# Gated linear attention and a gated convolution layer on one Trainium2 core: low parts and state sums on TensorE, weights in twelve parts, unit rows padded to 128, a new plan

## The chip, the cores and the metric

The kernel runs on one core of one Trainium2 chip. The metric is device time in microseconds, the median of several executions. The core's engines work on their own instruction queues, each in order: TensorE (PE; its weight loads are shown apart as PEld), VectorE (DVE), ScalarE (ACT), GpSimd (POOL), and SyncE (SP), which here issues most DMAs.

## The reference

For each of 4 batches and 8 heads a state of 48 x 48 is carried along 768 steps. Its output y, the heads side by side, is the x (768 x 384) of the second half.

```python
state = alpha[:, :, t, :, None] * state + einsum('bhd,bhe->bhde', k[:, :, t], v[:, :, t])
y[:, :, t] = einsum('bhd,bhde->bhe', q[:, :, t], state)

h = maximum(x @ w_in, 0)                  # 384 -> 1024
conv[t] = cw[0]*h[t-1] + cw[1]*h[t] + cw[2]*h[t+1]   # zero outside
out = (h * sigmoid(conv)) @ w_out         # 1024 -> 384
```

## The kernel before

The attention is cut into chunks of 128 time steps: 24 steps (`attn`, L586), six for each batch. Heads are held in two groups of four, on rows 0 to 47 and 64 to 111. Units of one or two chunks are loaded (`load_unit`, L521) and prepared (`prep_unit`, L538) with scans that turn alpha into running products and multiply them into k and q; units 0 to 2 do these multiplies on VectorE, later ones on GpSimd. Units 0 and 1 are the first two chunks of batch 0, unit 2 its chunks 2 and 3, unit 3 its chunks 4 and 5.

A step makes scores `a`, masks them into `at`, transposes k to `kt`, forms the state's update `u`, adds the old state and multiplies by a decay into `sc`, and makes `yp` from `at`, v and the old state. The masks come in three forms (L602 to L616): A multiplies the late half by a mask on VectorE and cuts the early half with two triangles on GpSimd; B multiplies both halves on VectorE (four products, no triangle); C copies on ScalarE and cuts all with four triangles. Before, steps 0 to 3 have form C, 4 and 5 form B, the rest A.

The layer's products run in fp32r with split operands: a value is a high part plus a low part. For x, ScalarE copies the high part out of `yp` and VectorE subtracts it for the low part (L670, L671). Six gathers `x<-x` on SP (L680) then complete the rows of x for a unit.

The weights come as 64-bit floats, in 8 parts of 768 words for each row, two of them staged at a time in `wscr`, which holds one of the two `x2` buffers that batches use. `to_parts` (L684) turns a part into float32 with two ScalarE operations, a clamp, a mask and a shift on VectorE, and an integer add on GpSimd; ScalarE casts the high part, and VectorE (parts 0 to 3) or GpSimd (4 to 7) subtracts it.

The layer (`moe_piece`, L730) works on pieces of 384 time steps, 8 tiles of 128 columns of `w_in` each: nine matmuls `ph`, relu on ScalarE into `h`, the three taps (one on ScalarE, two on VectorE), sigmoid, the product `gf` on VectorE, its high part `g` on ScalarE and low part on GpSimd, then nine matmuls `po`. The first piece needs steps 0 to 3. A `po` result leaves through `ob` and a DMA.

The order on each engine is made by a planner (`Plan.schedule`, L161): it goes through a model of costs, takes the operation of lowest rank among those that could start, and lets no operation start whose rank is over WINDOW (32) above the lowest open one. Ranks come from a formula of turns (L904 to L921) with some values set by hand (L957 to L970). Where the plan leaves TensorE empty before the first `po`, it puts filler matmuls `junk` on zeros (`keep_warm`, L450).

Of the kernel before, what the change touches and what calls it, by code (L numbers as in the profile page):

```python
# [94 lines left out]
class Op:  # L95
    __slots__ = ("eng", "fn", "cost", "lat", "port", "rank", "preds", "succs", "need", "bufs", "allocs", "start", "end", "seq", "xfer", "name", "mode", "base")
# [5 lines left out]
class Plan:  # L102
    ENGINES = ("PE", "DVE", "ACT", "POOL", "SP")

    def __init__(self, window, tol=0.05):
        self.classes = {}
        self.window, self.tol = window, tol
        self.memory = {}
        self.ops, self.bufs = [], []
        self.rank = 0.0  # L110
        self.gap_fill = None
# [16 lines left out]

    def const(self, shape, name, dt=None):

        self.pool(name, 1, int(np.prod(shape[1:])))
        return self.buf(name, shape, name, dt)


    def op(self, eng, fn, reads, writes, cost, port=False, xfer=0.0, name="", mode=None):
# [3 lines left out]
        o.preds, o.succs, o.bufs, o.allocs = set(), [], [], []  # L139
# [170 lines left out]
class Engines:  # L310
# [49 lines left out]
    def act(self, out, a, func, scale=1.0, bias=0.0, accum=None):  # L360
        n = out.n
        cost = (n + 195) / 1200 + (0.1 if isinstance(scale, View) else 0.0) + (0.19 if accum is not None else 0.0)
# [99 lines left out]
def record(nc, akq, akqu, v, vu, wts, out):  # L462
# [27 lines left out]
    plan.pool("small", 4, 48)  # L490
# [9 lines left out]
    ident = plan.const([P, P], "ident")  # L500
    ones = plan.const([R, 1], "ones")
# [13 lines left out]
    def unit_rows(u):  # L515
        b, t0, TU = units[u]
        n = 3 * G * TU
        off = (b * S + t0) * 3 * G * R
        return akqu[off : off + R * n].rearrange("(r x) -> r x", r=R)

    def load_unit(u):  # L521
        b, t0, TU = units[u]
        r = plan.buf("raw", [R, 3 * G * TU], f"akq_{u}")
        L = G * TU
        if u == 0:
            for a in (1, 0, 2):
                cols = slice(a * L, (a + 1) * L)
                E.dma("SP", r[:, cols], unit_rows(u)[:, cols], R * L * 4 / 1000)
        else:
            E.dma("SP", r, unit_rows(u), R * 3 * L * 4 / 1000)  # L530
# [7 lines left out]
    def prep_unit(u, qm, km, am):  # L538
# [4 lines left out]
        flat = raw[u]  # L543
# [32 lines left out]
    def chunk(b, c):  # L576
        u, ci = unit_of[(b, c)]
        TU = units[u][2]
        kq = raw[u].rearrange("p (a t) -> p a t", a=3 * G)
# [6 lines left out]
    def attn(si, form, kte):  # L586
        b, c = steps[si]
        u, ci, ks, qs, vf = chunk(b, c)
        nm = f"{b}_{c}"
        late, early = slice(0, HC), slice(HC, C)  # L590
# [27 lines left out]
        if c < NC - 1:  # L618
            kt_ps = plan.buf("mm", [P, G, R], f"ktp_{nm}", kind="kt")
            E.transposes([(kt_ps[:, g, :], ks[:, g, :]) for g in range(G)], ident[0:R, 0:R], 0.87, f"kt {nm}")  # L620
# [4 lines left out]
            for g in range(G):  # L625
                todo.append((up[0:64, g, :], kt[:, g, 0:64], vf[:, g * D : (g + 1) * D], g == 0, g == G - 1))
                todo.append((up[64:R, g, :], kt[:, g, 64:R], vf[:, (g + G) * D : (g + G + 1) * D], g == 0, g == G - 1))
# [10 lines left out]
        plan.rank += OUT_LAG  # L638
        old = state.get(b)
        yps = []  # L640
        for half in range(2):
            yp = plan.buf("mm", [R, 2, C], f"yp{half}_{nm}", kind="yp")
            for i in range(2):
                g, flip = PAIRS[2 * half + i]
                hs = (g + G, g) if flip else (g, g + G)
                last = c == 0 and i == 1
# [6 lines left out]
        if c > 0:  # L653
            todo = []
            for n in (0, 2, 1, 3):
                yp, i, g, flip = yps[n]
                for j in range(2):
                    rows = slice(64 * j, 64 * j + D)
                    o = 64 * (1 - j) if flip else 64 * j
                    todo.append((yp[o : o + D, i, :], old[rows, g, :], qs[rows, g, :], False, i == 1))  # L660
# [6 lines left out]
        for half in range(2):  # L667
# [3 lines left out]
            E.tt("DVE", at_[:, :, 1, ts], yp[:, :, ::-1], at_[:, :, 0, ts], ALU.subtract)  # L671
# [9 lines left out]
        plan.rank -= OUT_LAG  # L681


    def to_parts(raw64, hi, lo, tmp, full=None, eng="DVE"):  # L684

        lw, hw = raw64[..., 0] if False else raw64[0], raw64[1]
        d, r = tmp
# [7 lines left out]
        if full is not None:  # L695
            E.tt("POOL", full.bitcast(I32), di, ri, ALU.add)
            return
        E.tt("POOL", di, di, ri, ALU.add)
        E.copy("ACT", hi, d)
        E.tt(eng, lo, d, hi, ALU.subtract)  # L700

    WP = 768

    def load_weights(ranks, los):
        w64 = None if wts is None else wts.bitcast(U32).rearrange("p (n two) -> p n two", two=2)
        cut = (lambda a, e: None) if wts is None else (lambda a, e: w64[:, a:e])
        craw = plan.buf("small", [P, 3 * NF, 2], "craw", U32)
        plan.rank = ranks[0]
        E.dma("ACT", craw, cut(8 * WP, 8 * WP + 3 * NF), 24)
        scr = plan.buf("x2", [P, 8, WP], "wscr")  # L710
        for j in range(8):
            plan.rank = ranks[j]
            stg = scr[:, 2 * (j % 2) : 2 * (j % 2) + 2].rearrange("p a w -> p (a w)").bitcast(U32).rearrange("p (w two) -> p w two", two=2)
            tmps = [scr[:, 4 + 2 * (j % 2)], scr[:, 5 + 2 * (j % 2)]]
            i = j // 2 if j % 2 == 0 else 4 + j // 2
            E.dma("SP", stg, cut(i * WP, (i + 1) * WP), 786)
            if j == 0:
                to_parts((craw[:, :, 0], craw[:, :, 1]), None, None, [t[:, 0 : 3 * NF] for t in tmps], full=cw.rearrange("p a f -> p (a f)"))
            if i < 4:
                cs = slice(256 * i, 256 * i + 256)  # L720
                dst = [w[:, :, cs] for w in wi]
                v3 = lambda t: t.rearrange("p (t f) -> p t f", t=3)
                s3 = stg.rearrange("p (t f) two -> p t f two", t=3)
                to_parts((s3[:, :, :, 0], s3[:, :, :, 1]), dst[0], dst[1], [v3(t) for t in tmps], eng=los[j])
            else:
                dst = [w.rearrange("p f m -> p (f m)")[:, (i - 4) * WP : (i - 3) * WP] for w in wo]
                to_parts((stg[:, :, 0], stg[:, :, 1]), dst[0], dst[1], tmps, eng=los[j])
# [303 lines left out]
```

## Time and profile before

| | us |
|---|---|
| median of 3 runs | 364.61 (364.14 to 364.99) |
| profiled execution, first to last instruction (span) | 360.8 |
| TensorE, weight loads, VectorE, ScalarE, GpSimd busy | 330.9, 304.6, 260.5, 231.9, 189.5 |

The profiled execution's own time is its span and what lies around it before the first and after the last instruction; it is not listed apart from the runs. Busy TensorE includes 33.1 us of `junk`. A wait is put down to the engine that came last. The chain of waits is followed back from the last instruction of a stretch. Busy times in a table by stage are merged, so that instructions that overlap count once.

### The profile page before, as it was taken

What the parts mean: (1) busy time and instruction counts of PE and PEld (TensorE: products, weight loads), DVE (VectorE), ACT (ScalarE), POOL (GpSimd) and SP (SyncE); (2) the same over time, 40 slices, a digit from 0 to 9 for tenths busy, and PEclk for the clock granted to TensorE, in tenths of its full rate; (3) what the DMA queues carried; (4) which work ended last, traced back from release to release, by engine and by line L of the source; (5) the groups of instructions that cost most, each with busy time, mean ns of one, the idle gap of its engine ahead of it and who ended that gap; (6) DMA issues with size and microseconds to landing.
All of it is one profiled execution on the core that took longest, in us unless ns stands there. A gap on an engine that the chain in (4) does not pass through costs nothing.

```text
span 360.8 us, 8874 instructions
## 1 busy us (share of the span) xinstructions
PE 330.9 (92%) x3518; PEld 304.6 (84%) x3518; DVE 260.5 (72%) x475; ACT 231.9 (64%) x471; POOL 189.5 (53%) x228
## 2 busy tenths in 40 slices
PE   8899978986999997999899997999999999999971
PEld 8779867876989877998699985999998788999961
DVE  6799799956979578876988745765978845573631
ACT  2766647775587655968585673784886666576641
POOL 3338954595756673575557746361677421423420
PEclk9999999999899998999999998999999999999998
DMA  7985396069210076301800635740100011101002
GB/s 202 272 220 184 101 281 190 8 189 260 54 65 3 3 220 195 90 0 51 233 6 3 191 95 144 187 109 2 66 2 3 16 40 58 22 1 67 0 2 77
DMA packets 12339, 35.30 MB, mean 98 GB/s; under 512 B 2352, under 2 KB 8176, under 8 KB 11056
## 3 DMA queue, kind: packets, MB, share of 16 engines
q1 hardware_dynamic: 9120, 30.48, 31.2%
q10 hardware_dynamic: 3168, 4.15, 3.2%
q8 instruction: 30, 0.49, 0.6%
q14 instruction: 21, 0.17, 0.1%
HBM read 27.55 MB, written 4.72 MB: 89 GB/s over the span
## 4 chain that ended last, share of the span: by engine, by line
PE 56%; DVE 10%; ACT 10%; POOL 9%; issue 6%; DMA 4%; SPq 2%; ACTq 1%; POOLq 0%; DVEq 0%
PE ph L412 21%; PE po L412 21%; PE yp L412 6%; PE a L412 4%; POOL at L401 3%; DVE ph L335 3%; POOL wscr L329 3%; DMA akq<-in_akqu_dram 2%; PE u L412 2%; ACT at L353 2%; DVE suf L383 2%; SPq L426 2%; DMA x<-x 2%; POOL akq L329 2%; ACT wscr L371 1%
## 5 line engine op out<-in xcount | busy, mean ns | idle before, releaser
L412 PE MATMUL ph<-x,wi 128*128 128x386 f32 x576 | 112.0, 347 | 6.6 <-DVE gf L329 3.2
L412 PE MATMUL po<-wo,g 128*128 128x384 f32 x576 | 110.2, 341 | 3.1 <-ACT g L353 1.6
L412 PEld LDWEIGHTS ph<-x,wi 128*128 128x128 f32 x576 | 104.2, 193 | 8.8 <-DVE gf L329 4.0
L335 DVE SCALAR_TENSOR_TENSOR ph<-h,cw,ph 128x384 f32<-128x384 f32 x128 | 78.3, 620 | 44.6 <-ACT ph L376 37.1
L412 PEld LDWEIGHTS po<-wo,g 128*128 128x128 f32 x576 | 100.4, 189 | 6.6 <-POOL g L329 2.9
L329 POOL TENSOR_TENSOR g<-gf,g 128x384 fp32r<-128x384 f32 x64 | 73.2, 1150 | 45.3 <-ACT g L353 45.0
L401 POOL TENSOR_SCALAR_AFFINE_SELECT at<-at 64x256 f32<-64x256 f32 x52 | 35.8, 704 | 33.5 <-ACT at L353 32.5
L371 ACT ACTIVATE h<-ph 128x386 f32<-128x386 f32 x64 | 31.2, 488 | 29.1 <-PE ph L412 26.0
L329 DVE TENSOR_TENSOR gf<-h,ph 128x384 f32<-128x384 f32 x64 | 35.0, 548 | 13.7 <-ACT ph L371 13.3
L371 ACT ACTIVATE ph<-ph 128x384 f32<-128x384 f32 x64 | 30.0, 470 | 14.5 <-DVE ph L335 13.4
L376 ACT ACTIVATE ph<-h,cw 128x384 f32<-128x384 f32 x64 | 37.4, 584 | 1.4
L353 ACT CAST g<-gf 128x384 fp32r<-128x384 f32 x64 | 32.0, 508 | 8.6 <-DVE gf L329 6.8
L353 ACT COPY at<-a 64x512 f32<-64x512 f32 (+1 forms) x56 | 27.1, 537 | 12.7 <-DVE at L329 8.6
L412 PE MATMUL yp<-at,v 128*48 128x128 f32 (+1 forms) x384 | 30.4, 285 | 5.2 <-POOL at L401 2.9
L452 PE MATMUL junk<-idle 128*128 128x128 bf16 x492 | 33.1, 230 | 1.0 <-POOL idle L379 1.0
L452 PEld LDWEIGHTS <-idle 128*128 128x128 bf16 x492 | 30.5, 104 | 2.8 <-issue 1.6
L412 PEld LDWEIGHTS yp<-at,v 128*48 128x48 f32 (+1 forms) x384 | 22.4, 132 | 11.5 <-POOL at L401 5.2
L329 POOL TENSOR_TENSOR akq<-akq,pre 112x1024 f32<-112x1024 f32 x10 | 23.8, 2381 | 13.2 <-DVE pre L383 13.1
L329 POOL TENSOR_TENSOR akq<-akq,suf 112x1024 f32<-112x1024 f32 x10 | 24.6, 2458 | 10.1 <-DVE suf L383 7.1
L383 DVE TENSOR_TENSOR_SCAN pre<-akq,d1f 112x1024 f32<-112x1024 f32 (+1 forms) x13 | 28.3, 2178 | 0.0
L329 DVE TENSOR_TENSOR x<-yp,x 112x256 fp32r<-112x256 f32 x48 | 18.0, 415 | 14.0 <-ACT x L353 13.7
L383 DVE TENSOR_TENSOR_SCAN suf<-akq,e_last 112x1023 f32<-112x1023 f32 (+1 forms) x13 | 27.6, 2123 | 0.3
(67 smaller groups left out, 326.4 us busy)
## 6 DMA issues: line engine op xcount, KB each, us to landing
akq<-in_akqu_dram SPq DMA_DIRECT2D x11, 1344.0 KB, 9.0
wscr<-in_wts_dram SPq DMA_DIRECT2D x8, 768.0 KB, 4.7
v<-in_vu_dram SPq DMA_DIRECT2D x11, 384.0 KB, 9.2
out_dram<-ob ACTq DMA_DIRECT2D x21, 192.0 KB, 1.9
x<-x SPq DMA_DIRECT2D x66, 32.0 KB, 3.0
akq<-in_akqu_dram SPq DMA_DIRECT2D x3, 224.0 KB, 3.1
akq<-in_akqu_dram SPq DMA_DIRECT2D x1, 672.0 KB, 7.7
out_dram<-ob SPq DMA_DIRECT2D x3, 192.0 KB, 3.1
```

The lines of the kernel that those rows point to most:

```text
L329: self.plan.op(e, lambda: self.eng(e).tensor_tensor(A(out), A(a), A(b), op=op), [a, b], [out], cost, port, name=f"tt {out.buf.name}")
L335: "DVE", lambda: self.nc.vector.scalar_tensor_tensor(A(out), A(a), A(s), A(b), o0, o1),
L353: fn = lambda: self.nc.scalar.copy(A(out), A(a))
L371: self.nc.scalar.activation(A(out), A(a), func, **k)
L376: self.plan.op("ACT", lambda: self.nc.scalar.mul(A(out), A(a), A(s)), [a, s], [out], (out.n + 320) / 1200, name=f"mul {out.buf.name}")
L383: "DVE", lambda: self.nc.vector.tensor_tensor_scan(A(out), A(a), A(b), init, o0, o1), [a, b], [out],
L401: lambda: self.nc.gpsimd.affine_select(out=A(out), in_=A(out), pattern=pattern, compare_op=ALU.is_ge, fill=0.0, base=base, channel_multipl ...
L412: self.nc.tensor.matmul(A(out), A(w), A(x), start=start, stop=stop, skip_group_check=True)
L426: e, lambda: self.eng(e).dma_start(A(out), A(a)), [a], [out], 0.35 if e == "ACT" else 0.7, xfer=max(kb / rate, 0.02),
L452: nc.tensor.matmul(junk[:, 0:128], zero, zero, start=True, stop=True)
```

## The change

- The low part of x of steps 0 to 5 is made on TensorE: `yp` gets a further matmul with minus the identity (`neg`) on the high part, and ScalarE copies the rest out. Later steps keep VectorE.
- The state sum of steps 0 to 5 (where there is an old state) is a further matmul into `u`; VectorE then makes the product alone.
- Weights come in 12 parts of 512 words, staged three deep, in an order of their own (WORDER). Parts 0 to 5 in that order have their low part made on TensorE and copied by ScalarE, the others on VectorE. The clamp of every second part is on GpSimd.
- Units are loaded with 128 rows, 16 of them zeros, and work on 112 as before.
- The last tile of the last piece goes through its chain in three pieces of 128 columns, its low part on VectorE.
- Forms: B in step 0, C in 1 and 2, A after. Ranks are a table with one entry for each group of operations, WINDOW is 80.8, and some costs of the planner's model are changed.

```diff
+    neg = plan.const([P, P], "neg", F32R)
+        r = plan.buf("raw", [P, 3 * G * TU], f"akq_{u}")
+            E.dma("SP", r, unit_rows(u), P * 3 * L * 4 / 1000)
...
-            E.transposes([...], ident[0:R, 0:R], 0.87, f"kt {nm}")
+            E.transposes([...], ident[0:R, 0:R], 0.45, f"kt {nm}")
...
+            if c > 0 and SUM[si] == "PE":
+                E.mm([(up, ident[0:R, 0:R], state[b], False, True)], 0.35, f"sum {nm}")
-            if c == 0:
+            if c == 0 or SUM[si] == "PE":
                 E.tt("DVE", sc, up, pcb, ALU.mult)
             else:
                 E.tt("DVE", tmp, up, state[b], ALU.add)
                 E.tt("DVE", sc, tmp, pcb, ALU.mult)
...
             E.copy("ACT", at_[:, :, 0, ts], yp[:, :, ::-1])
-            E.tt("DVE", at_[:, :, 1, ts], yp[:, :, ::-1], at_[:, :, 0, ts], ALU.subtract)
+            if XLO[si] == "PE":
+                E.mm([(yp, neg[0:R, 0:R], at_[:, :, 0, ts][:, :, ::-1], False, True)], 0.15, f"xlo {nm}")
+                E.copy("ACT", at_[:, :, 1, ts], yp[:, :, ::-1])
+            else:
+                E.tt("DVE", at_[:, :, 1, ts], yp[:, :, ::-1], at_[:, :, 0, ts], ALU.subtract)
...
-        E.ts("DVE", d, d, F64_LO, F64_HI, ALU.max, ALU.min)
+        E.ts(eng, d, d, F64_LO, F64_HI, ALU.max, ALU.min)
...
-    WP = 768
+    WP = 512
+    NW = NF * DM // WP
+        scr = plan.buf("x2", [P, 12, WP], "wscr")
+        for j in range(2 * NW):
+            q = 4 * (j % 3)
+            di, ri = to_f32(stg[:, :, 0], stg[:, :, 1], d, r, WMASK[j])
+            E.tt("POOL", di, di, ri, ALU.add)
+            E.copy("ACT", hi, d)
+            if WLO[j] == "PE":
+                pl = plan.buf("mm", [P, WP], f"wl_{j}", kind="wl")
+                E.mm([(pl, ident, d, True, False), (pl, neg, hi, False, True)], 1.1, f"wlo {j}")
+                E.copy("ACT", lo, pl)
+            else:
+                E.tt(WLO[j], lo, d, hi, ALU.subtract)
...
+            end = last and f == NF - 1
+            for a0, a1 in ENDCUT if end else ((0, n),):
+                (relu, taps, sigmoid, gf, g high as before, on columns a0 to a1)
+                E.tt("DVE" if end else "POOL", g[:, 1, cs], gf[:, cs], g[:, 0, cs], ALU.subtract)
...
-WINDOW = 32
-OUT_LAG = 1.23
-WLO = ["DVE"] * 4 + ["POOL"] * 4
-FORM = lambda si: "C" if si < 4 else "B" if si < 6 else "A"
+ENDCUT = ((0, 128), (128, 256), (256, 384))
+WINDOW = 80.8
+RANKS = {"load": [...], "prep": [...], "scores": [...], "state": [...], "out": [...], "weights": [...], "up": [...], "down": [...]}
+WORDER = [0, 1, 6, 2, 3, 7, 8, 4, 5, 9, 10, 11]
+WLO = ["PE"] * 6 + ["DVE"] * 6
+WMASK = ["DVE", "POOL"] * 6
+FORMS = "BCCAAAAAAAAAAAAAAAAAAAAA"
+XLO = ["PE"] * 6 + ["DVE"] * 18
+SUM = ["PE"] * 6 + ["DVE"] * 18
```

## Rows read from the trace of the kernel before

**Rows 1.** Three stages: start:end, length, busy us of PE, PEld, DVE, ACT, POOL, clock, DMA share, GB/s.

```profile
8.10:56.00 47.90, 42.00 (x783) 36.43 (x781) 41.72 (x70) 31.35 (x59) 27.46 (x25) 1.00 0.76 207
56.00:100.00 44.00, 38.83 (x280) 36.81 (x281) 35.73 (x59) 30.00 (x58) 30.50 (x27) 0.96 0.51 140
100.00:345.00 245.00, 236.55 (x2353) 219.50 (x2352) 172.10 (x325) 165.00 (x345) 126.70 (x159) 0.99 0.24 69
```

**Rows 2.** The same stages, PE busy with the tile `junk` alone.

```profile
8.10:56.00 47.90, 23.74 (x379) 1.00 0.76 207
56.00:100.00 44.00, 2.30 (x38) 0.96 0.51 140
```

**Rows 3.** The chain of waits from 28 to 57 us: start, us, what.

```profile
30.06 1.77 POOL wscr L329
...
37.24 2.91 POOL at L401
...
40.23 2.00 POOL wscr L329
42.23 3.04 POOL akq L329
...
50.47 5.50 DMA x<-x
```

**Rows 4.** Tiles `at`, `wscr`: ns least/median/most of one, first and last start.

```profile
L401 POOL TENSOR_SCALAR_AFFINE_SELECT at<-at x52: 407/416/2903, 11.4 to 294.8; 64x256 f32<-64x256 f32 x52
...
L329 POOL TENSOR_TENSOR wscr<-wscr x8: 1829/2063/3740, 30.1 to 82.8; 128x768 int32<-128x768 int32 x8
...
L329 POOL TENSOR_TENSOR wo<-wscr,wo x2: 1802/1815/1828, 76.6 to 85.6; 128x768 fp32r<-128x768 f32 x2
```

**Rows 5.** Timeline at 56 us: start, us, engine, line, operation, count, idle before.

```profile
56.00 4.29 PE L412 MATMUL ph<-x,wi 128*128 128x386 f32 x23 [1.72 <-DMA x<-x]
```

**Rows 6.** Groups of instructions from 0 to 100 us: count, busy us, mean ns, idle before.

```profile
L401 POOL TENSOR_SCALAR_AFFINE_SELECT at<-at 64x256 f32<-64x256 f32 x16 | 13.6, 870 | 15.5 <-ACT at L353 15.2
...
L345 DVE TENSOR_SCALAR wscr<-wscr 128x768 f32<-128x768 f32 x8 | 4.5, 558 | 0.9 <-ACT wscr L371 0.8
L329 DVE TENSOR_TENSOR x<-yp,x 112x256 fp32r<-112x256 f32 x12 | 4.4, 411 | 2.1 <-ACT x L353 2.1
L353 ACT COPY at<-a 64x512 f32<-64x512 f32 x8 | 4.4, 581 | 0.1
...
L353 ACT CAST x<-yp 112x256 fp32r<-112x256 f32 x12 | 3.9, 377 | 2.6 <-PE yp L412 2.5
...
L329 DVE TENSOR_TENSOR sc<-st,p_c 112x192 f32<-112x192 f32 x4 | 3.1, 766 | 0.0
L329 DVE TENSOR_TENSOR at<-a,mask 64x256 f32<-64x256 f32 x8 | 3.0, 414 | 0.1
...
L329 DVE TENSOR_TENSOR st<-u,sc 112x192 f32<-112x192 f32 x4 | 1.4, 349 | 0.0
```

**Rows 7.** From 0 to 100 us, `wscr` alone: busy us of DVE, ACT, POOL.

```profile
0.00:100.00 100.00, 26.24 (x31) 21.42 (x26) 25.71 (x13) 0.98 0.65 177
```

**Rows 8.** Timeline at 45 us, four transposes.

```profile
45.32 0.60 PE L420 MATMUL ktp<-ident,akq 112*128 112x112 f32 x4 [0.64 <-POOL akq L329]
```

**Rows 9.** DMA issues: count, KB each, median us from issue to landing.

```profile
akq<-in_akqu_dram SPq DMA_DIRECT2D x11, 1344.0 KB, 9.0
wscr<-in_wts_dram SPq DMA_DIRECT2D x8, 768.0 KB, 4.7
```

**Rows 10.** A short stretch, columns as in rows 1.

```profile
88.00:92.10 4.10, 4.10 (x16) 4.10 (x15) 3.81 (x11) 3.87 (x10) 2.26 (x6) 0.58 0.92 232
```

**Rows 11.** Timeline of the last tile.

```profile
347.26 0.49 ACT L371 ACTIVATE h<-ph 128x386 f32<-128x386 f32 x1 [0.17 <-PE ph L412]
...
351.52 1.00 POOL L329 TENSOR_TENSOR g<-gf,g 128x384 fp32r<-128x384 f32 x1 [1.64 <-ACT g L353]
...
352.58 1.50 PE L412 MATMUL po<-wo,g 128*128 128x384 f32 x7 [0.46 <-POOL g L329]
```

More of the change, by code (lines that the diff above doesn't have):

```diff
@@ L95 @@
 class Op:
-    __slots__ = ("eng", "fn", "cost", "lat", "port", "rank", "preds", "succs", "need", "bufs", "allocs", "start", "end", "seq", "xfer", "name", "mode", "base")
+    __slots__ = ("eng", "fn", "cost", "lat", "port", "rank", "preds", "succs", "need", "bufs", "allocs", "start", "end", "seq", "xfer", "name", "mode", "base", "group")
 SWITCH = 0.1
@@ L109, in __init__ @@
         self.ops, self.bufs = [], []
-        self.rank = 0.0
+        self.rank, self.group = 0.0, None
         self.gap_fill = None
@@ L127, in buf, with at @@
         return View(b, idx, 0, shape[0], ())
+    def at(self, key, *i):
+        t = RANKS[key]
+        for k in i:
+            t = t[k]
+        self.rank, self.group = t, (key,) + i
     def const(self, shape, name, dt=None):
@@ L618, in attn @@
         if c < NC - 1:
+            plan.at("state", si)
             kt_ps = plan.buf("mm", [P, G, R], f"ktp_{nm}", kind="kt")
-            E.transposes([(kt_ps[:, g, :], ks[:, g, :]) for g in range(G)], ident[0:R, 0:R], 0.87, f"kt {nm}")
+            E.transposes([(kt_ps[:, g, :], ks[:, g, :]) for g in range(G)], ident[0:R, 0:R], 0.45, f"kt {nm}")
             kt = plan.buf("kt", [P, G, R], f"kt_{nm}")
@@ L636, in attn @@
                 E.tt("DVE", sc, tmp, pcb, ALU.mult)
-        plan.rank += OUT_LAG
+        plan.at("out", si)
         old = state.get(b)
@@ L694, in to_parts, with load_weights @@
         E.act(ri, lw, AF.Copy, scale=2.0**-29)
[L695 to L700, printed above, removed]
-    WP = 768
-    def load_weights(ranks, los):
+        return di, ri
+    WP = 512
+    NW = NF * DM // WP
+    def load_weights():
         w64 = None if wts is None else wts.bitcast(U32).rearrange("p (n two) -> p n two", two=2)
@@ L731, in moe_piece @@
+    def moe_piece(x, to, s0, s1, b, rank, last=False):
         n = s1 - s0
@@ L742, in moe_piece @@
         for f in range(NF):
-            plan.rank = rank(f)
+            rank("up", f)
             nm = f"{b}_{s0}_{f}"
@@ L897, in record @@
     E.memset("POOL", ones, 1.0)
+    E.act(neg, ident, AF.Copy, scale=-1.0)
     def ready_pieces(b, c):
         return [(s0, s1) for s0, s1 in PIECES[b] if min(s1, S - 1) // C == c]
-    turn, t, n_tiles = [], 0.0, 0
-    tiles, credit = [], 0.0
-    avail = 0
-    for si, (b, c) in enumerate(steps):
-        turn.append(t)
-        t += 4.0
-        credit += RATE if len(tiles) >= N0 else RATE0
-        while credit >= 1.0 and len(tiles) < avail:
-            tiles.append(t)
-            t += 3.0
-            credit -= 1.0
-        if len(tiles) >= avail:
-            credit = min(credit, 1.0)
-        avail += NF * len(ready_pieces(b, c))
-    while len(tiles) < avail:
-        tiles.append(t)
-        t += 3.0
-    plan.turns = (turn, tiles)
     first = {}
@@ L927, in record @@
     n_piece = 0
-    for u in range(2):
-        plan.rank = -90.0
-        load_unit(u)
-    load_weights(WRANK, WLO)
+    load_unit(0)
+    load_unit(1)
+    load_weights()
     for si, (b, c) in enumerate(steps):
-        u, ci = unit_of[(b, c)]
         for sj in {0, si + 1} if si == 0 else {si + 1}:
```

137 lines of the change are left out of this document (68 added, 69 removed), and 17 rows, old and new, of the table RANKS.

## Prediction

> **What bounds the kernel now.** I read the table by stages first, then the filler matmuls in the same stages, then the chain of waits, then groups and single tiles where the chain stops. The table [rows 1] cuts the span where the work changes: until 56.0 the attention steps and the weights prepare the first `ph` group, until 100 the weights are finished beside the first tiles, then TensorE works through batches. From 100 to 345 TensorE is busy 236.6 of 245 us: it is the bound there, with 8.4 us idle. From 8.1 to 56 it reads 42.0 of 47.9 us, but 23.7 us of that is `junk`, the filler that keeps it awake [rows 2]. With 5.9 us idle, 29.6 of the 47.9 us hold no work of the kernel. From 56 to 100 it is 5.2 us idle plus 2.3 us of junk. So the prize is early, and the question is which engine holds TensorE up there. VectorE is busy 41.7 of 47.9 us in the first of these stages, the highest share of any engine but TensorE, and GpSimd is what the chain runs over: from 30.06 to 45.3 us nearly each piece of the chain is GpSimd, a weight part's add, the triangles of steps 2 and 3, another add, unit 3's k multiply [rows 3]. The two are one bound: a triangle takes 407 to 416 ns when it runs undisturbed and 2.9 us at worst, an add 1.83 us at best and 3.74 at worst [rows 4]; the long ones stand where VectorE is full. At the end of that chain the six gathers `x<-x` take 5.5 us to land, and `ph` begins at 56.00 [rows 3, 5].
>
> **The sum's frame.** The profiled execution's own time is its span, 360.8 us, and what lies around it. The runs' median is 364.61 (364.14 to 364.99), so 3.8 us lie around it; I take the profiled execution as one of these and sum against 364.6.
>
> **VectorE's relief, counted.** (a) The low parts of x of steps 0 to 5 leave VectorE: 12 x 0.411, whose merged busy time is 4.4 us [rows 6]. (b) The state sums of steps 1 to 4 leave it (step 5 has none): the add (349 ns) goes, and the product after it reads PSUM, which the row of the add prices at 349 instead of 766 ns; 4 x (0.349 + 0.766 - 0.349) = 3.1 us. (c) Weights: 26.2 us of VectorE [rows 7]. The words stay (8 x 768 = 12 x 512), and VectorE keeps half of the low parts' words as now. A fixed part of 0.15 us per instruction follows from 414 ns at 256 and 349 at 192 elements [rows 6]; four more parts of two instructions and two more low parts cost 10 x 0.15 = 1.5 us, and of the clamps (max, then min; 4.5 us now, [rows 6]) half the words move to GpSimd, which gives back some 2. Net -0.5. (d) Forms: step 0 goes from C to B (four masked products more), step 3 from C to A (two more), steps 4 and 5 from B to A (two fewer each): 2 x 0.414 = +0.8. Together -7.2 us, of which the x parts of steps 0 to 3 (2.9) and three sums (2.3) lie ahead of the first `ph`.
>
> **What it adds elsewhere.** ScalarE: 12 more instructions on the weights at a fixed 0.17 us (581 ns at 512 elements against 377 at 256, [rows 6]) are 2.0, six low parts read from PSUM 6 x 0.58 = 3.5, twelve low parts of x 12 x 0.377 = 4.5; less about 1 us by the forms, so +9 us on 62 us of work in the first 100 (the stages of [rows 1] hold 61.4). Its cover is the idle third of ScalarE; without that cover all 9 us would be late. The added wait is ScalarE's copy of a low part waiting for TensorE, and behind it stand the next tile's relu and the kt copies. GpSimd: four low parts of 1.81 us go (-7.2); four more adds pay a fixed part, between nothing and a whole triangle (0.41), so 0 to 1.6, and I take 1; six clamps of 512 come, which the trace doesn't show: 0.81 by the undisturbed triangle (0.407 at 256) and 1.22 by the add (1.83 at 768, [rows 4]), so +4.9 to +7.3, undisturbed; triangles of steps 0 to 5 go from 16 to 14 (-1.7 by their mean of 0.87). Net -3 to -0.6, I take -2. TensorE: a weight low part is a pass of 512 through `neg` (0.187 at 386, so 0.25, [rows 5]) and one of full float32, between 0.25 and 0.69 (0.60 for four of 112, [rows 8]); I take 0.6, as the transposes are the same kind of matmul. Six are 3.0 to 5.6, twelve x parts of 256 columns 1.5, four sums 0.4 to 1.0: 5 to 8 us in all. They cost nothing as long as they fall into the 29.6 us without work; were that gone, they would cost all of it. Queue SP issues four more weight loads, and three staging places instead of two let it stand less before a full one. Unit loads grow from 1344 to 1536 KB: by bytes the 9.0 us to landing become up to 10.3, while a weight load of 128 rows takes 4.7 for 768 KB [rows 9], so a faster rate isn't excluded; -1 to +1.3 on a load, mostly ahead of need, and I put it at nothing.
>
> A move in the change that a rule speaks against is the clamp on GpSimd. The rows show triangles and adds between 0.41 and 2.9 and between 1.83 and 3.74 us [rows 4]. The Trainium skill, "SBUF — State Buffer", section "SBUF: two separate sides", says that VectorE and GpSimd lock one port pair against each other for a whole instruction, the loser standing still. The trace agrees, with 2903 against a median of 416 ns. By that rule the six clamps, which I count as a relief of 2 us, may hold VectorE up for their own 5 to 7 us, and the sum would be that much worse.
>
> **Stage by stage.** Up to the first `ph`: the triangles of step 3 halve (two fewer at 0.41 to 2.91 each, [rows 3, 4]; nearer the middle in a stretch where VectorE is full, so 2.6), the add ahead of them shrinks by a third of its 1.8 (0.6), and unit 3's multiply (3.04) and the second add (2.00) need not precede the gathers, since the first `ph` reads steps 0 to 3 (units 0 to 2) only. That is up to 8.2 on GpSimd, beside 5.2 on VectorE; they overlap, and the gathers' landing stays. I take -8, with bounds -2 (the order uses neither) and -15 (half of the 29.6). From 56 to 100: 7.5 us of TensorE hold no work, and a dip of the granted clock (mean 0.58 over 4.1 us, nearly all of it at 1.2 GHz, [rows 10]) costs 1.7 more; with the rest of the relief I take -3, bounds +3 (TensorE's added work and ScalarE's 9 us show) and -7. From 100 to 345: 8.4 us idle and, by the mean clock of 0.99, 2.5 us of clock; a planning window of 80.8 instead of 32 and a rank for each group let another tile stand where TensorE waits. I take half, -5, bounds +3 and -9. What is late next there is VectorE, 172 of 245 us, so it still covers. Tail: the last tile goes from its relu (347.26) to its last `po` group (352.58) in 5.3 us, 1.00 of it the low part on GpSimd, and `po` then needs 1.5 [rows 11]. In three pieces with the low part on VectorE the chain keeps near 5 us, since each piece pays the fixed parts again, but two thirds of the `po` work run beside it: -1.5, bounds 0 and -2.5.
>
> Sum: -8 - 3 - 5 - 1.5 = -17.5, so **347 us**. Its own range, with the terms partly off together, is 340 to 353.
>
> **Rivals.** *Only the counted relief arrives* (358): the order gives nothing by itself, and the engines stay in step with VectorE until 100, so the early gain is 5 of the 7.2 us and the tail's 1.5. For it: VectorE stands at 87% before 56 and 81% after; against it speaks a chain that names pieces which the first `ph` doesn't need. Chance 0.22. *The order fills nearly everything* (331): -15 - 7 - 9 - 2.5 = -33.5. For it: idle and junk are there to be had; against it: ScalarE's 9 us and waits that a plan doesn't foresee. Chance 0.13. *The port turns it over* (371): the plan gives 12 adds and 6 clamps their undisturbed prices, and instructions behind them run in order. If all 18 were held as the worst add was (3.74 - 1.83 = 1.9 each) GpSimd would lose 34 us; adds and low parts lose 4 now (25.7 in [rows 7] against 8 x 1.83 + 4 x 1.81 = 21.9). At 24 us on the chain toward the first `ph` and the weights, the sum is 364.6 - 17.5 + 24 = 371. It decides the sign from 17.5 us on. Against it: GpSimd is busy only 27.5 of 47.9 and 30.5 of 44 us [rows 1]. Chance 0.10. *Nothing that can be told* (364.6): gains and the 5 to 8 us of new TensorE work cancel; 0.04.
>
> **How the numbers follow.** The forecast holds the remaining 0.51. Faster by over 0.2% (about what a measurement of this kernel can tell from no change): 0.51 + 0.22 + 0.13 = 0.86; same 0.04; slower 0.10. The range goes from 334, which keeps a part of the filled order, to 361, which takes in the counted relief and its bounds; outside lie the port rival and the far end of the filled order, under 0.2.
>
> **What would show it.** Right, if the first `ph` starts at 45 to 51 us and not 56; if VectorE's `wscr` time in the first 100 us stays at 24 to 28 us and the clamps on GpSimd take 0.8 to 1.3; if junk falls under 20 us; if TensorE's idle time from 100 on falls to about 4 us; if the last relu to the last `po` piece takes 5 us with little `po` behind it. Wrong, if triangles and adds at 2 to 4 us hold the chain again, if ScalarE passes 90% before 100, if the low parts' copies on ScalarE wait for TensorE, or if the clock falls to 1.2 GHz more often once the first `po` has ended the filler.

## The result and the profile after

The kernel after takes 351.49 us (median of 4 runs, 349.07 to 353.80) against 364.80 us of the kernel before beside it; the ratio is 0.9637, 95% interval 0.9556 to 0.9719. Ratios, here and below, leave out executions over 1.5% longer than the fastest of the same kernel, which the medians keep. The forecast was 347.0 with a range of 334 to 361. The four runs lie in two pairs, 349.1 and 349.4 at a mean granted clock of 0.997 and 0.998, 353.6 and 353.8 at 0.991 and 0.983; the profiled one is 353.6 us long, with a span of 351.4. So 2.2 us lie around the span. Where the kernel before was run again, its span of 360.8 went with 362.5 us. The profiled execution of before was thus about 2 us under its median, and the one of after about 2 us over its own, so from profile to profile the gain is 9.4 us, from median to median 13.3.

Of the page of after, the span and the busy time of each engine:

```profile
span 351.4 us, 8817 instructions
...
PE 328.8 (94%) x3481; PEld 302.4 (86%) x3481; DVE 259.4 (74%) x478; ACT 241.4 (69%) x506; POOL 186.9 (53%) x231
```

The table by stages of after, columns as in [rows 1]; the last three stages are cut at the last tile's relu (336.71) and at the end of the last `po` (345.41):

```profile
8.10:56.00 47.90, 42.67 (x659) 35.90 (x660) 34.64 (x61) 33.47 (x71) 28.87 (x23) 1.00 0.56 198
56.00:100.00 44.00, 42.67 (x365) 38.96 (x364) 36.56 (x63) 36.97 (x78) 33.14 (x34) 1.00 0.45 170
100.00:336.71 236.71, 227.96 (x2324) 213.23 (x2323) 177.53 (x326) 164.15 (x342) 120.94 (x157) 0.99 0.22 76
336.71:345.41 8.70, 8.42 (x45) 7.47 (x43) 4.14 (x14) 4.08 (x15) 1.02 (x1) 1.00 0.05 19
```

The same cuts of before, from 100 us to its last relu (347.26) and on to the end of its last `po` (354.08):

```profile
100.00:347.26 247.26, 238.77 (x2364) 221.37 (x2362) 173.43 (x328) 165.67 (x347) 126.70 (x159) 0.99 0.24 68
347.26:354.08 6.82, 4.22 (x18) 2.93 (x18) 2.99 (x6) 2.91 (x7) 2.00 (x2) 1.00 0.02 4
```

The filler `junk` of after alone, in its first two stages:

```profile
8.10:56.00 47.90, 20.42 (x295) 1.00 0.56 198
56.00:100.00 44.00, 2.47 (x32) 1.00 0.45 170
```

With [rows 1, 2] these rows give the time in which TensorE does none of the kernel's work, that is the stretch less what is busy, plus the junk:

| stage | before | after | difference |
|---|---|---|---|
| 8.1 to 56 | 29.6 | 25.7 | -4.0 |
| 56 to 100 | 7.5 | 3.8 | -3.7 |
| 100 to the last relu | 8.5 | 8.8 | +0.3 |
| last relu to the end of the last `po` | 2.6 | 0.3 | -2.3 |
| from there to the end of the span | 6.7 | 6.0 | -0.7 |

The first 8.1 us give another -0.3, and TensorE's time on work rises by 1.4 (busy less junk, 330.9 - 33.1 to 328.8 - 29.6). That closes the 9.4 us. It has to be read with care in the first two stages: the change puts new work on TensorE there, and new work lowers the time without work while it brings the end no nearer. How far ahead the old work is, another cut shows. Before, then after, from 345 us on:

```profile
345.00:361.00 16.00, 6.44 (x31) 4.80 (x29) 4.67 (x9) 4.11 (x10) 2.00 (x2) 0.92 0.13 45
```

```profile
345.00:352.00 7.00, 0.42 (x3) 0.10 (x1) 0.36 (x1) 0.32 (x1) 0.00 (x0) 0.76 0.28 95
```

Before still has 6.44 us of matmuls to do and ends 15.8 us later, after 0.42 and 6.4. So 6.0 of the 9.4 us are a lead in work (work done earlier by the same moment) and 3.4 are less idle time at the end. Set side by side by the issue times of the same matmuls, the lead is 2.7 us at 100 and grows by some 3 until 345. The granted clock is a part of it: the dip of [rows 10] is gone (1.7 us), and from 100 to 345, summing one minus the granted clock over stretches of 5 us, before loses 3.4 us and after 1.7. The same measure over the whole span (one minus the mean granted clock, times the span: the most that the clock can have cost) holds for every run on record. It is 0.7 to 6.0 us in the four runs of after, 2.7 in the mean, and 8.1 to 9.5 in the mean of the runs of before that were taken beside the experiments. So up to about 6 of the 13.3 us between the medians are clock.

### The profile page after: what moved, and what is told of

The parts are those of the page before. It is cut to its first block, busy times and chain, and to the rows that moved or that the text cites. A ratio compares the mean times of both kernels' runs of the same rounds, so it can differ in the third digit from the quotient of the medians.

```text
span 351.4 us, 8817 instructions
## 1 busy us (share of the span) xinstructions
PE 328.8 (94%) x3481; PEld 302.4 (86%) x3481; DVE 259.4 (74%) x478; ACT 241.4 (69%) x506; POOL 186.9 (53%) x231
## 4 chain that ended last, share of the span: by engine, by line
PE 63%; DVE 15%; ACT 7%; issue 4%; DMA 4%; POOL 4%; ACTq 0%; SPq 0%; DVEq 0%; POOLq 0%
PE po L418 23%; PE ph L418 22%; PE yp L418 7%; PE a L418 4%; DMA x<-x 4%; DVE ph L341 4%; PE u L418 3%; PE junk L458 2%; DVE pre L389 2%; PE ktp L426 2%; POOL at L407 2%; ACT akq L377 2%; POOL wscr L351 2%; DVE sc L335 1%; DVE gf L335 1%
## 5 line engine op out<-in xcount | busy, mean ns | idle before, releaser
L341 DVE SCALAR_TENSOR_TENSOR ph<-h,cw,ph 128x384 f32<-128x384 f32 (+1 forms) x132 | 78.0, 606 | 36.6 <-ACT ph L382 30.9
L407 POOL TENSOR_SCALAR_AFFINE_SELECT at<-at 64x256 f32<-64x256 f32 x50 | 29.8, 607 | 40.1 <-ACT at L359 38.8
L377 ACT ACTIVATE h<-ph 128x386 f32<-128x386 f32 (+1 forms) x66 | 31.5, 479 | 16.4 <-PE ph L418 13.4
L335 DVE TENSOR_TENSOR gf<-h,ph 128x384 f32<-128x384 f32 (+1 forms) x66 | 33.8, 533 | 8.7 <-ACT ph L377 7.8
L377 ACT ACTIVATE ph<-ph 128x384 f32<-128x384 f32 (+1 forms) x66 | 30.5, 463 | 14.1 <-DVE ph L341 13.0
L382 ACT ACTIVATE ph<-h,cw 128x384 f32<-128x384 f32 (+1 forms) x66 | 37.9, 575 | 2.4 <-DVE ph L341 0.8
L359 ACT CAST g<-gf 128x384 fp32r<-128x384 f32 (+1 forms) x66 | 31.8, 500 | 9.1 <-DVE gf L335 5.6
L458 PE MATMUL junk<-idle 128*128 128x128 bf16 x417 | 29.6, 225 | 1.0 <-POOL idle L385 1.0
L385 POOL MEMSET h<- 128x1 f32 x64 | 5.6, 99 | 45.5 <-DVE gf L335 41.1
L418 PE MATMUL a<-akq 48*64 48x128 f32 (+1 forms) x768 | 26.4, 250 | 2.9 <-DVE gf L335 1.5
L458 PEld LDWEIGHTS <-idle 128*128 128x128 bf16 x417 | 25.5, 101 | 4.0 <-issue 2.2
```

The lines of the kernel that those rows point to most:

```text
L335: self.plan.op(e, lambda: self.eng(e).tensor_tensor(A(out), A(a), A(b), op=op), [a, b], [out], cost, port, name=f"tt {out.buf.name}")
L341: "DVE", lambda: self.nc.vector.scalar_tensor_tensor(A(out), A(a), A(s), A(b), o0, o1),
L359: fn = lambda: self.nc.scalar.copy(A(out), A(a))
L377: self.nc.scalar.activation(A(out), A(a), func, **k)
L382: self.plan.op("ACT", lambda: self.nc.scalar.mul(A(out), A(a), A(s)), [a, s], [out], (out.n + 320) / 1200, name=f"mul {out.buf.name}")
L385: self.plan.op(e, lambda: self.eng(e).memset(A(out), x), [], [out], 0.06 + out.n * 1e-3, e == "POOL", name=f"set {out.buf.name}")
```

## The experiments

Two kinds follow. In the first the source is changed and the planner makes the order anew. In the second ("plan kept") each engine's order stays that of the kernel after, operation by operation, and only what an operation issues, or on which engine, is changed; these begin with `clamp_fixed`, the run behind "Clamps back, plan kept". Ratios are to the kernel before, run beside them; "us against after" is the difference of two such ratios times 364.8. Each such difference carries about 4 us either way at 95%, most of it from the four runs of after, which all the differences share. The edits are shown shortened; "..." marks what is left out.

**All parts, the old ranks.** The formulas of turns and WINDOW 32 in place of the table.

```diff
-WINDOW = 80.8
...
+WINDOW = 32
...
-RANKS = {"load": [...], ...}
+RANKS = (load, prep, steps, tiles by the formulas of the kernel before)
```

> All parts of the change, but the ranks by the formulas and the window of 32 of the kernel before; the twelve weight parts take the eight old weight ranks in rising order. Theory that the order made the gain: 358 to 366 us, little or nothing better than the kernel before. Theory that the parts made it, the order a little: 349 to 355 us.

385.53 us, ratio 1.0559 (1.0477 to 1.0641). Both expectations were too low by about 20 us and more: with the old formulas the parts are slower than before, not worth their counted relief. From 56 to 100 TensorE is busy 36.4 of 44 us, 10.55 of them junk.

**Clamps back, planned anew.**

```diff
-WMASK = ["DVE", "POOL"] * 6
+WMASK = ["DVE"] * 12
```

> All twelve clamps on VectorE, same ranks, planned again. Theory that the six clamps on GpSimd (1.98 us each in the changed kernel's trace, two of them back to back at 40.8 us on the chain to the first ph) cost time: 347 to 350 us, the first ph 1 to 3 us earlier than 52.8. Rival that VectorE needs the relief of 2 us: 352 to 355 us.

378.40 us, ratio 1.0368 (1.0284 to 1.0453). Both theories missed it, by over 20 us.

**Low parts and sums back, planned anew.**

```diff
-XLO = ["PE"] * 6 + ["DVE"] * 18
-SUM = ["PE"] * 6 + ["DVE"] * 18
+XLO = ["DVE"] * 24
+SUM = ["DVE"] * 24
```

> Low parts of x and the state sums of all steps on VectorE again, same ranks, planned again. Theory of the prediction, that VectorE's relief of 7.5 us by these two carries the early gain: 355 to 359 us, the first ph 3 to 5 us later than 52.8. Rival, since VectorE is busy 34.6 of 47.9 us before 56 in the changed kernel: 350 to 353 us.

390.24 us, ratio 1.0660 (1.0568 to 1.0753), outside both expectations too.

**Units of 112 rows, planned anew.**

```diff
-            r = plan.buf("raw", [P, 3 * G * TU], f"akq_{u}")
+            r = plan.buf("raw", [R, 3 * G * TU], f"akq_{u}")
...
-            E.dma("SP", r, unit_rows(u), P * 3 * L * 4 / 1000)
+            E.dma("SP", r, unit_rows(u), R * 3 * L * 4 / 1000)
```

> Unit loads of 112 rows again, the rest of the change kept, planned again with its transfers a seventh smaller. Theory that the faster loads count (421 GB/s at a full share in the changed kernel's trace against 272 before): 353 to 358 us, loads in the first 20 us back near 270 GB/s. Rival that loads lie ahead of need: 350.5 to 352.5 us.

394.65 us, ratio 1.0773 (1.0683 to 1.0863), again outside both. Four kernels, four losses of 27 to 41 us against after, whatever was undone. That pointed to what they have in common, a plan that the table of ranks wasn't made for.

**The same parts, ranks rounded.** Nothing is undone here; each rank is rounded to a whole number.

```diff
-        self.rank, self.group = t, (key,) + i
+        self.rank, self.group = float(round(t)), (key,) + i
```

> The changed kernel with each rank rounded to a whole number, planned again; engines, sizes and parts unchanged. Theory that the table of ranks is worth something only where every tie and near tie falls as it was tuned: 358 to 385 us, and as slow as the runs that were planned again (378 to 395). Rival that the ranks carry a robust order: 350 to 354 us.

394.41 us, ratio 1.0811 (1.0740 to 1.0882): 43 us from rounding alone, more than its theory allowed (385) and as slow as the runs planned anew. Two stretches of 20 us, columns as in [rows 1]:

```profile
80.00:100.00 20.00, 12.93 (x129) 10.64 (x129) 17.11 (x23) 10.78 (x25) 11.86 (x17) 0.91 0.19 54
240.00:260.00 20.00, 13.54 (x95) 12.46 (x94) 13.73 (x21) 8.29 (x17) 5.62 (x3) 0.68 0.50 178
```

TensorE stands 7.1 and 6.5 us in them, no engine but VectorE in the first is near full, and in the second the granted clock's mean is 0.68. So a kernel that is planned anew doesn't price the part that was undone, and the four runs above say nothing on it. What they suggest is that this table fits this set of parts and costs only. From here the plan is kept.

**Clamps back, plan kept.** The six clamps planned for GpSimd are issued to VectorE.

```diff
-            e, lambda: self.eng(e).tensor_scalar(...)
+            e, lambda: self.nc.vector.tensor_scalar(...)
```

> The changed kernel with its plan kept to the letter: each engine's operations in the planned order, but the six clamps that GpSimd had are issued to VectorE at the place in the plan where they stood. Theory that the clamps on GpSimd cost time: 347 to 350 us, first ph 1 to 3 us earlier than 52.8. Rival that VectorE needs the relief: 352 to 355 us. Against the run with the clamps on VectorE and a new plan (378 us), a time under 356 shows that the plan and not the clamps made that run slow.

349.04 us, ratio 0.9577 (0.9526 to 0.9629): 2.2 us under after, with intervals that overlap, and the lowest median of this study. Its chain of waits from 37 to 53 us (start, us, what):

```profile
37.09 3.45 PE wl L418 x9
40.54 0.07 PE junk L458
40.61 3.21 PE yp L418 x62
...
47.03 4.01 DMA x<-x
51.04 0.09 issue
51.13 2.18 PE ph L418 x11
```

GpSimd is out of the chain there, and `ph` begins 1.6 us earlier than in after (below). Both are as the first theory said.

**Low parts of x and sums back, plan kept.** The further matmuls aren't issued; VectorE adds the state ahead of the product, and subtracts the high part where ScalarE copied.

```diff
-E.mm([(up, ident[0:R, 0:R], state[b], False, True)], 0.35, f"sum {nm}")
-E.tt("DVE", sc, up, pcb, ALU.mult)
+nc.vector.tensor_tensor(sc, up, old, add); nc.vector.tensor_tensor(sc, sc, pcb, mult)
...
-E.copy("ACT", at_[:, :, 1, ts], yp[:, :, ::-1])
+nc.vector.tensor_tensor(lo, yp, hi, subtract)
```

> The changed kernel with its plan kept, but the low parts of x and the state sums of steps 0 to 5 are computed on VectorE at the places where ScalarE's copy and VectorE's product stood; the TensorE matmuls of these are not issued. Theory of the prediction that this relief of VectorE carries the early gain: 355 to 359 us. Rival that VectorE had slack for it: 350 to 353 us. Either is far under the 390 us of the run that was planned again, if the plan made that one slow.

358.22 us, ratio 0.9781 (0.9711 to 0.9850): 5.3 us against after, as the theory of the prediction had it. The profiled execution is a longer one, of 360.6 us, with `ph` from 53.9. Its first stage, columns as in [rows 1]:

```profile
8.10:56.00 47.90, 40.58 (x652) 33.80 (x650) 39.71 (x72) 31.10 (x62) 25.55 (x21) 0.98 0.50 182
```

VectorE has 39.7 us of work where after has 34.6. That these 5.1 us and the 5.3 at the end are about equal shows no cause: the first `ph` comes only 1.1 us later than in after, and a good part of the rest is clock (at the end of this section).

**Units of 112 rows, plan kept.** The loads' sizes and the host's layout alone.

```diff
-        off = (b * S + t0) * 3 * G * P
+        off = (b * S + t0) * 3 * G * R
...
-            r = plan.buf("raw", [P, 3 * G * TU], f"akq_{u}")
+            r = plan.buf("raw", [R, 3 * G * TU], f"akq_{u}")
```

> The changed kernel with its plan kept, unit loads of 112 rows instead of 128. Theory that the faster loads of 128 rows count: 354 to 360 us, GB/s between 10 and 20 us back near 270. Rival that loads lie ahead of need: 350 to 353 us. The run that was planned again took 395.

356.27 us, ratio 0.9784 (0.9725 to 0.9843): 5.4 us against after. The stretch from 10 to 20 us, where unit loads fill the queues, with parts of the weights and v between them, columns as in [rows 1] with the DMA share and GB/s last. Before:

```profile
10.00:20.00 10.00, 8.93 (x179) 7.91 (x180) 8.36 (x20) 7.03 (x18) 5.16 (x7) 1.00 1.02 272
```

After:

```profile
10.00:20.00 10.00, 7.72 (x118) 6.96 (x117) 8.95 (x17) 5.23 (x11) 4.90 (x3) 1.00 1.02 421
```

After's plan with 112 rows:

```profile
10.00:20.00 10.00, 8.80 (x148) 7.55 (x146) 7.66 (x15) 6.25 (x14) 4.93 (x3) 1.00 1.01 267
```

At the same full share of the DMA engines, the stretch moves 267 to 272 GB/s with unit loads of 112 rows and 421 with 128. The first `ph` starts at 53.5 us here, 0.7 later than in after, and as late in `tail_whole`, which has 128 rows and the same plan up to its end. So the 5.4 us are not lost there. In the profiled execution (356.2 us) most of them lie from 136 to 148 us. After, then this run:

```profile
136.00:148.00 12.00, 11.71 (x157) 10.38 (x150) 8.49 (x20) 7.16 (x16) 4.06 (x5) 1.00 0.84 310
```

```profile
136.00:148.00 12.00, 11.65 (x138) 10.11 (x139) 6.56 (x18) 5.11 (x12) 2.83 (x9) 0.57 0.77 207
```

The granted clock is 0.57 instead of 1.00, which costs up to 5.2 us. Just before it TensorE stands three times, for 1.66, 0.30 and 0.52 us, and in after at the same matmuls for 1.59, 0.31 and 0.51. Why the clock falls behind the one and not behind the other isn't seen, and `xsum_fixed` and `clamp_wlo_fixed` have the same dip (0.51 and 0.50) with 128 rows. So it isn't shown that slower loads cost these 5.4 us.

**Before, with 128 rows and its own plan kept.** The one part alone, from the other side.

```diff
-        off = (b * S + t0) * 3 * G * R
+        off = (b * S + t0) * 3 * G * P
...
-            r = plan.buf("raw", [R, 3 * G * TU], f"akq_{u}")
+            r = plan.buf("raw", [P, 3 * G * TU], f"akq_{u}")
```

> The kernel before with its plan kept, unit loads of 128 rows instead of 112; nothing else. Theory that the faster loads count by themselves: 358 to 363 us. Rival that the old plan doesn't wait for loads: 363.5 to 366 us.

358.94 us, ratio 0.9889 (0.9842 to 0.9936): -4.0 us against before, and the interval lies below 1. Its tile `ph` (least, median, most ns; first and last start in us):

```profile
L412 PE MATMUL ph<-x,wi x576: 332/339/526, 52.7 to 342.6; 128*128 128x386 f32 x192
```

The first `ph` starts at 52.7 us, as in after, without any of the moves between engines and without the new plan. VectorE's first work on the second unit (start, us; idle before it in brackets), in before, then here:

```profile
10.35 0.17 DVE L357 COPY ast<-akq 112x4 f32<-112x4 f32 x1 [2.21 <-DMA akq<-in_akqu_dram]
```

```profile
8.50 0.17 DVE L357 COPY ast<-akq 112x4 f32<-112x4 f32 x1 [0.40 <-DMA akq<-in_akqu_dram]
```

Over the whole run VectorE stands 3.5 us at this line before and 0.7 here: the old plan did wait for its loads.

**Weights' low parts back on VectorE, plan kept.** The subtraction stands at the matmuls' place in the order; their copies on ScalarE aren't issued.

```diff
-                E.mm([(pl, ident, d, True, False), (pl, neg, hi, False, True)], 1.1, f"wlo {j}")
-                E.copy("ACT", lo, pl)
+                nc.vector.tensor_tensor(lo, d, hi, subtract)
```

> The changed kernel with its plan kept, but the six weight low parts that TensorE makes are subtracted on VectorE at the place in the plan where the matmuls stood; neither these matmuls nor ScalarE's six copies are issued. Theory that VectorE is still short of time up to 56 us: 353 to 356 us. Rival, since ScalarE loses 3.5 us of copies and VectorE stands idle from 40 to 60 us: 348 to 351 us.

356.72 us, ratio 0.9797 (0.9733 to 0.9862): 5.8 us against after, 0.7 over the theory that VectorE is still short there; the other, that the copies on ScalarE cost more than they bring, falls. The profiled execution, a short one of 353.0 us, is no longer than the one of after, so it doesn't show the whole loss, but it shows how VectorE's work gets through to TensorE. The first `ph` is no later (52.2), but TensorE waits (its timeline, idle before in brackets):

```profile
43.84 0.64 PE L418 MATMUL yp<-x,neg 112*112 112x256 f32 x2 [2.79 <-ACT x L359]
...
62.23 1.98 PE L418 MATMUL a<-akq 48*64 48x64 f32 x32 [3.58 <-DVE gf L335]
```

From 40 to 45 us VectorE is busy without a gap (2.99 of 5 us in after). In after the first of these matmuls doesn't wait and the second waits 0.35 us. Behind each wait the granted clock falls, to 0.62 from 44 to 48 us and 0.63 from 60 to 68, where after keeps 1.00:

```profile
60.00:68.00 8.00, 5.77 (x59) 5.20 (x60) 6.62 (x13) 4.32 (x9) 5.78 (x6) 0.63 0.58 213
```

The 7 us of TensorE work that this run leaves out are gone from the same stretch, so whether VectorE's load or TensorE's missing work brought the clock down isn't told apart.

**Both: clamps and weights' low parts on VectorE, plan kept.**

> The same with the six clamps of GpSimd issued to VectorE too, at their places in the plan. If both edits gain by themselves they add up: 345 to 348 us. If VectorE has become the one that is short: 350 to 354 us, over the 349 us of the clamps alone.

353.02 us, ratio 0.9692 (0.9643 to 0.9741), in the range of the expectation that VectorE is the one that is short. Against `clamp_fixed` putting the weights' low parts back costs 4.2 us, against after 5.8; the clamps back on VectorE gain 2.2 with the low parts on TensorE and 3.8 without. The sizes agree within their intervals, and the lowest median has the low parts on TensorE and the clamps on VectorE.

**The last tile whole, low part on GpSimd.** The plan stays but for its last 44 of 1927 operations.

```diff
-ENDCUT = ((0, 128), (128, 256), (256, 384))
+ENDCUT = ((0, 384),)
-                E.tt("DVE" if end else "POOL", g[:, 1, cs], ...)
+                E.tt("POOL", g[:, 1, cs], ...)
```

> The changed kernel with the last tile's chain in one piece and its low part on GpSimd; planned again, and the plan is the same but for the last 44 of 1927 operations. Theory of the prediction, 1.5 us for the three pieces: 352 to 354 us. Rival that po work behind the chain covers it: 350.5 to 352 us.

351.70 us, ratio 0.9682 (0.9632 to 0.9732): +1.6 us against after, with intervals that overlap, and in the range of the rival that `po` work covers the chain. Its timeline from the last tile's relu on (start, us, engine, line, operation, count, idle before):

```profile
333.85 8.11 PE L418 MATMUL po<-wo,g 128*128 128x384 f32 x45
...
334.05 0.49 ACT L377 ACTIVATE h<-ph 128x386 f32<-128x386 f32 x1
...
338.34 1.01 POOL L335 TENSOR_TENSOR g<-gf,g 128x384 fp32r<-128x384 f32 x1 [3.18 <-ACT g L359]
```

The uncut chain is done at 339.35, 5.3 us after its relu, and 36 `po` of earlier tiles keep TensorE busy until after that. Relu to the last `po`'s end takes 7.9 us, against 8.7 in after, for the same 45 matmuls.

**The clock in the runs with the plan kept.** One minus the mean granted clock, times the span, is the most that the clock can have cost a run (the 30 `a` matmuls at 136 us take 1.10 us in after and 1.98 in `rows112_fixed`, at a clock of about a half). The mean over the runs that the ratios rest on, in us:

| kernel | against after | most that the clock cost |
|---|---|---|
| after | 0 | 2.7 |
| `clamp_fixed` | -2.2 | 1.9 |
| `tail_whole` | 1.6 | 3.1 |
| `xsum_fixed` | 5.3 | 4.7 |
| `rows112_fixed` | 5.4 | 6.6 |
| `wlo_fixed` | 5.8 | 9.3 |
| `clamp_wlo_fixed` | 2.0 | 7.7 |

So the whole loss of `wlo_fixed`, most of that of `rows112_fixed` and some of that of `xsum_fixed` can be clock. These runs price a part together with the clock dips that came with undoing it, and no run holds the clock fixed.

## Why the prediction was right or wrong

The sign, the range and the order of size held: 351.5 in 334 to 361, with 347 forecast. The sum behind it held much less, and that the number came out as near as it did is in part luck: the sum is -17.5 us, against -9.4 between the two profiles, and early and middle terms that were too large stand beside a padding and a tail that were too small. Of the signs that it named for being right, only VectorE's `wscr` time came as said.

**The frame.** I took 3.8 us around the span and so set the profiled execution at the median. It is 2.2 in after and 1.7 in the run of before that has the same span. The profiled execution was one of 362.5 us, so my -17.5 meant 345, and the -9.4 between the two profiles is what each stage is to be held against.

**What bounds the kernel.** VectorE and GpSimd as "one bound" early was half right. Low parts and sums put back on VectorE cost 4 to 6 us at the end (`xsum_fixed`, `wlo_fixed`, `clamp_wlo_fixed` against `clamp_fixed`), six clamps put back cost nothing, so a part of VectorE's relief mattered. But it didn't do so by holding up the first `ph`, which moves by no more than 1.1 us in these runs; what the trace of `wlo_fixed` shows is waits of TensorE further on and a lower granted clock behind them. And I had no term for the loads, and on the kernel before they alone bring the first `ph` from 56.0 to 52.7.

**Up to the first `ph`, -8: wrong in size.** It came 3.2 us earlier, at 52.77, not at 45 to 51. The chain of waits of after, start, us, what:

```profile
36.71 4.05 POOL at L407 x3
40.77 0.08 issue
40.84 1.97 POOL wscr L351
42.82 0.02 issue
42.84 1.10 DVE wscr L341
...
43.96 0.69 ACT wscr L377
44.65 1.07 ACT x L359 x4
45.72 0.58 ACT wscr L377
...
47.39 5.29 DMA x<-x
```

Against [rows 3] unit 3's multiply and the second add are indeed gone from it, but three triangles (4.05 us together) and a clamp stand in their place, and behind the clamp ScalarE's work on a weight part and copies of x in turn. The forecast named this as its "wrong": triangles and adds that hold the chain again. The wait behind the clamp falls away in `clamp_fixed`, where `ph` starts at 51.13 and so just misses the forecast's 45 to 51 as well. That the padding alone reaches 52.7 from the other side says that the GpSimd work ahead of it, which I took for the term, was not the only thing that held it; the wait for the unit loads was another.

**VectorE's relief: right as a count.** VectorE's time on `wscr` in the first 100 us is 25.05 us, forecast 24 to 28 (columns: PE, PEld, DVE, ACT, POOL):

```profile
0.00:100.00 100.00, 6.28 (x12) 2.10 (x12) 25.05 (x39) 23.91 (x38) 29.13 (x19) 1.00 0.53 189
```

VectorE falls from 41.7 to 34.6 us before 56. ScalarE rises by 9.1 us in the first two stages, as counted (+9), and doesn't pass 90% (70.4 of 91.9 us). GpSimd was to lose 2 us and gained 4.0 in the same stages, and its `wscr` time went from 25.71 [rows 7] to 29.13.

**The clamp on GpSimd: a price that failed.** Tile `wscr` on GpSimd, ns least/median/most:

```profile
L335 POOL TENSOR_TENSOR wscr<-wscr x12: 1265/1285/1822, 13.4 to 87.9; 128x512 int32<-128x512 int32 x12
L351 POOL TENSOR_SCALAR wscr<-wscr x6: 1913/1922/2225, 10.0 to 83.4; 128x512 f32<-128x512 f32 x6
```

I bounded it by 0.81 (triangle) and 1.22 us (add), and it takes 1.92, six of them 11.8 instead of 4.9 to 7.3. Both rows were other operations, and a bound "from the nearest rows" should have gone beyond the upper one; why a clamp takes more than an add no run shows. Six clamps on VectorE would have been 3.1 us (0.52 each, the mean of the six that stay there), so moving them cost GpSimd nearly four times what it bought. In `clamp_fixed` VectorE's first stage rises by 1.9 us, to 36.55, and its second by 3.2. The port isn't seen to have made the clamps dear: the longest of the six is 2225 ns against 1913 at best, a stretch of 0.3 us. So the rule that VectorE and GpSimd lock a shared port pair against each other (the Trainium skill, "SBUF — State Buffer", section "SBUF: two separate sides") doesn't show in them. Triangles do stretch, to 2773 ns against a median of 416, as before.

**The rival of the port** (371) did not come: adds of 512 run at 1.29 us, 1.82 at worst, far from 1.9 us more each, and the kernel is faster.

**TensorE's new work: under-counted.** The weights' passes take 7.17 us (merged) where I had 3.0 to 5.6, the low parts of x 3.1 where I had 1.5, the sums 2.1 where I had 0.4 to 1.0: 12.4 us for 5 to 8. A weight part is three records that overlap in part, two of 0.592 us for the float32 pass and one of 0.79 for the high part. They did fall into the time without work, as I said; what I missed is that such cover is then spent, and that time without work is not the same as gain. Of 7.7 us less of it before 100, only 2.7 became a lead. Junk is 29.6 us in all of after, not under 20.

**The padding at nothing: wrong.** The step that failed is "mostly ahead of need": VectorE stood 3.5 us for unit loads, and 0.7 with 128 rows. I had the clue in [rows 9]: 768 KB of 128 rows in 4.7 us are 163 KB/us, 1344 KB of 112 rows in 9.0 are 149, and I wrote that a faster rate isn't excluded. But these are times to landing, which hold the queue. The row that would have raised the question is the rate of a stretch where the DMA engines are full, 272 GB/s before, beside such a stretch with 128 rows. It is worth 4.0 us on before, against 0 in the sum; undone in after it costs 5.4, most of which can be clock.

**From 56 to 100, -3: right in size.** 3.7 us less without work, and the dip of [rows 10] is gone, 1.7 more; new TensorE work takes part of it back.

**From 100 to 345, -5: half right, by another way.** Idle time doesn't fall (8.5 to 8.8; forecast about 4). What comes is 1.7 us of clock and a lead that the early stages left. One wait of after remains (TensorE's timeline; idle before it in brackets):

```profile
221.73 1.24 PE L418 MATMUL yp<-at,v 128*64 128x128 f32 x14 [2.64 <-issue]
```

Right behind it the granted clock has a mean of 0.57 over 4 us, so that most of them run at the lower level, 1.2 GHz:

```profile
222.00:226.00 4.00, 4.00 (x51) 3.91 (x48) 2.01 (x7) 0.89 (x3) 0.00 (x0) 0.57 0.74 249
```

In `clamp_fixed`, with the same order, the same wait is 1.27 us and the clock stays at 1.00:

```profile
218.44 0.97 PE L418 MATMUL yp<-at,v 128*64 128x128 f32 x14 [1.27 <-issue]
```

Why TensorE waits there isn't seen in the trace and stays open. The runs of after at 349 us have the clock of 0.997, so this dip is a likely, not a shown, reason for their two pairs, and a part of `clamp_fixed`'s 2.2 us may be that dip and not the clamps.

**Tail, -1.5: right in sign, too small, for the wrong reason.** It gave 3.0 us (2.3 before the last `po`'s end, 0.7 after). I put it on the three pieces, with two thirds of the `po` work beside them. `tail_whole` has the chain uncut and TensorE without a gap through it, since 36 `po` are left to run beside it; before, 18 matmuls of the last tiles ran in the same place, with 2.6 us idle. So what brought it is `po` work that the order keeps back for the end, and the pieces lengthen the chain (7.1 us from the first relu to the end of the last low part, against 5.3 whole, on ScalarE and VectorE in turn):

```profile
336.71 0.28 ACT L377 ACTIVATE h<-ph 128x131 f32<-128x131 f32 x1
...
343.53 0.29 DVE L335 TENSOR_TENSOR g<-gf,g 128x128 fp32r<-128x128 f32 x1 [0.36 <-ACT g L359]
```

Whether the pieces gain anything at the end the intervals leave open.

**The rivals.** "Only the counted relief" (358) and the forecast (347) lie 6.5 and 4.5 us from what came, so neither number tells. As mechanisms: its premise that "the order gives nothing by itself" can't be had apart from the parts, since any new plan from the table costs 27 to 43 us. With the plan kept, low parts and sums of x (5.3), low parts of the weights (5.8), padding (5.4) and the clamps (-2.2) add up to 14.3 us, where the whole gain is 13.3. The error of after's four runs enters that sum four times, so it is known to some 13 us only. Nor may it be read as an order worth nothing: the plan was made for all parts together, so each may cost more to undo than it brought, and the clock dips of these runs are in it. How much of the gain is the order's own stays open. The padding alone was tried from both sides (4.0 and 5.4).

## What to carry to other kernels

Where the order comes from a planner with fitted ranks, undo a part with the plan kept; a plan made anew prices the fit (rounding the ranks cost 43 us here) and not the part. Even then look at the granted clock of both runs before you call the difference the price of the part (`wlo_fixed` lost 5.8 us, and its clock alone can account for them). Time in which the bound engine does no work is a purse, not a gain: work moved into it costs little and empties it, so count the lead of the old work at a fixed moment instead. Before a larger transfer is put at nothing, read its rate in GB/s in a stretch where the DMA share is full, beside a transfer of another shape.

## What the runs showed of the hardware

A stretch filled by unit loads of 128 rows moved 421 GB/s in after, and one with 112 rows 267 (after's plan) to 272 (before), at a DMA share of 1.0 each time; the 14% more bytes of a unit landed no later (median 8.6 against 9.0 us). On GpSimd a float32 max and min with two constants over 128 x 512 took 1.92 us, an integer add of the same size 1.29; on VectorE the clamp took 0.52 us in the same kernel. The float32 pass with an identity over 512 columns shows as two records of 0.592 us each, against one of 0.79 us for the high part's pass. Waits of TensorE of nearly the same length (1.66 and 1.59 us) were followed by a granted clock of 0.57 over 12 us in one run (`rows112_fixed`) and of 1.00 in another (after).
